# A linear-attention and bilinear-FFN kernel: first scores moved ahead of the last k transposes, and the second kv update of a pair moved next to its intra products

## The chip, the cores and the metric

One core of a Trainium2 chip runs the whole program. The metric is the time of one execution on the device, in microseconds (us); a version is described by the median of its runs.

## The reference, cut to what matters

The first half is linear attention with a decay per head, over 4 sequences of 768 tokens, 8 heads of 64; the second half is a feed-forward layer that multiplies two projections.

```python
# per sequence b and head h, token i (state kv is 64 x 64)
#   out = (q k^T * decay_mask) v   +   q * lam^(i+1) @ kv          "intra" + "inter"
#   kv  = lam^block * kv + (k * decay)^T v                         "kv update"
x = out.transpose(0, 2, 1, 3).reshape(3072, 512)
a = x @ w_a          # 512 x 1536
b = x @ w_b
y = (a * b) @ w_out  # 1536 x 512
```

The kernel works in units of 128 tokens, 24 in all, six to a sequence. The powers of lam are multiplied into q and k beforehand, so that the mask is a plain triangle and the kv state a plain running sum in PSUM.

## The kernel before

The FFN runs over groups of units. The attention of later units is cut into pieces that are put, by a table of slots, between the FFN's matmuls: `P` scales and loads, `T` transposes, `S` makes scores and masks, `V` is a kv update with its copy, `Q` is two older units' products with the next two units' scores, `O2` the same without scores.

```python
for _g, _u in ((3, 11), (4, 15), (5, 19)):
    PLAN.setdefault(_g, []).extend(
        [(1, "V", _u - 1), (1, "P", _u + 2), (3, "P", _u + 3), (4, "V", _u),
         (7, "Q", (_u, _u + 1, _u + 2, _u + 3)), (10, "V", _u + 1), (10, "P", _u + 4),
         (12, "P", _u + 5), (13, "V", _u + 2), (16, "Q", (_u + 2, _u + 3, _u + 4, _u + 5))])
# ... cut ...
def ps_bank(name, shape, dt, hold=False, ffn=False):   # seven PSUM banks, taken in rotation
    i = bank["next"]
    while i in bank["held"] or (ffn and i == bank["ffn"]):
        i = (i + 1) % 7
    # ... cut: remember i, bank["next"] = (i + 1) % 7, return a tile in bank i
# ... cut ...
def mask(kq):                       # two score banks -> two masked bf16 tiles, on DVE
    for i in range(2):
        m = msk_pool.tile([128, HP, 128], BF16, name=f"m{i}", tag=f"m{i}")
        nc.vector.tensor_mul(m, kq[i], lotri_bc)
# ... cut ...
def kv_mms(ps, w, hps, first):      # four 128 x 128 matmuls, a pair of heads each
    d = U[w]
    for hp in hps:
        nc.tensor.matmul(ps[:, hp, :, :], lhsT=d["kn"][:, 2 * hp:2 * hp + 2, :],
                         rhs=d["vb"][:, 2 * hp:2 * hp + 2, :], ...)
def kv_copy(u, ps, eng="dve"):      # the state to bf16, only the diagonal 64 x 64 blocks
    st = st_bufs[u % 4]
    if eng == "act":
        for i in range(2):
            p = slice(64 * i, 64 * i + 64)
            nc.scalar.copy(st[p, :, i, :], ps[p, :, i, :])
    else:
        nc.vector.tensor_mul(st..., ps..., bdiag_bc)
# ... cut ...
def pieces_O(us, nxt=()):
    kqs = [score_banks() for u in nxt]
    for u in us:
        inter(u)
    for u, kq in zip(nxt, kqs):
        scores(u, kq)
    for u in us:
        intra(u)
        xT, col = xTs[u]
        evac_o(u, xT, col)
    for u, kq in zip(nxt, kqs):
        masks(u, kq)
# ... cut; the head, for the first four units:
scores4(0)                          # after all k transposes
natural_k((0, 1, 2), (0, 1)); warm(2)
natural_k((0, 1, 2), (2, 3)); warm(2)
scores4(1); warm(4)
sts = [ps_bank("kv0", ...), ps_bank("kv1", ...), kv_bank()]
for hh in range(2):
    for u, ps in enumerate(sts):
        ...                         # kv parts, state copies of 0 and 1 on ACT, of 2 on DVE
```

## Time and profile before

| | before |
|---|---|
| median of its runs | 237.72 us |
| span of the profiled execution | 235.4 us |
| busy share of PE, DVE, ACT, POOL | 96%, 49%, 39%, 21% |

PE is TensorE, PEld its weight loads, DVE VectorE, ACT ScalarE, POOL GpSimd. In a timeline, a row is a run of like instructions: start, length, engine, line and operation, the tile written and those read, shapes, count, and in brackets how long the engine sat idle before it and what ended that. The lines themselves stand in the prediction. The profiled execution took 237.14 us, 0.6 less than the median, which matters for differences of a few tenths.

### The profile page before, as it was taken

How to read it: one execution, taken by the hardware profiler on the slowest of the kernel's cores; microseconds unless marked ns; L12 is line 12 of the kernel's file. 1: busy time of each engine (PE TensorE's matmuls, PEld its weight loads, DVE VectorE, ACT ScalarE, POOL GpSimd, SP SyncE). 2: the span in 40 equal slices, each digit the busy share in tenths (PEclk: the TensorE clock that was granted, in tenths of full speed). 3: DMA queues.
4: the chain of work that ended last, by engine and by line, in shares of the span. 5: the costliest groups of instructions: out<-in, count | busy, mean ns of one | idle time of the engine just before them, and what ended most of it. 6: DMA issues, size and time to landing. Idle time of an engine off the chain costs nothing.

```text
span 235.4 us, 4530 instructions
## 1 busy us (share of the span) xinstructions
PE 225.1 (96%) x1755; PEld 126.2 (54%) x1778; DVE 115.7 (49%) x205; ACT 92.9 (39%) x174; POOL 49.4 (21%) x63
## 2 busy tenths in 40 slices
PE   7699999998999999999999999999999999999994
PEld 2475444448698654444544454544454544444493
DVE  0886566637469637565135665135564215332050
ACT  3567654065565542341142241242341242431161
POOL 6041000245346453103306403003300000000000
PEclk9999999999999999999999999999999999999999
DMA  4999999999999999998919959523120220000311
GB/s 153 301 287 349 349 367 284 292 213 286 204 234 204 223 183 257 183 187 152 242 72 220 177 70 239 140 77 79 26 47 0 89 89 5 0 0 3 133 46 49
DMA packets 94278, 38.32 MB, mean 163 GB/s; under 512 B 81200, under 2 KB 89776, under 8 KB 94256
## 3 DMA queue, kind: packets, MB, share of 16 engines
q1 hardware_dynamic: 94112, 38.02, 71.0%
q8 instruction: 14, 0.23, 0.4%
q14 instruction: 8, 0.07, 0.1%
q10 hardware_dynamic: 144, 0.00, 0.0%
HBM read 28.32 MB, written 6.29 MB: 147 GB/s over the span
## 4 chain that ended last, share of the span: by engine, by line
PE 85%; DMA 6%; DVE 2%; ACT 2%; issue 2%; SPq 1%; DVEq 0%; ACTq 0%
PE op L434 26%; PE a_ps L413 25%; PE b_ps L413 24%; DMA k<-in_k_dram 3%; DMA qkT<-qk 3%; PE o_ps L345 2%; PE kq L308 2%; DVE m L320 2%; PE kvd L359 2%; PE o_ps L335 1%; PE tps L294 1%; ACT xT L352 1%; ACT o_sb L429 1%; SPq L206 1%; ACT st L379 1%
## 5 line engine op out<-in xcount | busy, mean ns | idle before, releaser
L425 DVE TENSOR_TENSOR ab<-a_sb,b_ps 128x512 bf16<-128x512 bf16 (+2 forms) x96 | 52.7, 553 | 82.3 <-PE b_ps L413 61.2
L413 PE MATMUL a_ps<-xT,wa_sb 128*128 128x512 bf16 (+2 forms) x378 | 76.7, 325 | 1.6 <-DVE ab L425 0.6
L413 PE MATMUL b_ps<-xT,wb_sb 128*128 128x512 bf16 (+2 forms) x379 | 76.7, 325 | 0.2
L420 ACT CAST a_sb<-a_ps 128x512 bf16<-128x512 f32 (+2 forms) x96 | 45.6, 481 | 65.6 <-PE a_ps L413 63.4
L434 PE MATMUL op<-wo_sb,ab 128*128 128x512 bf16 (+2 forms) x300 | 64.2, 362 | 0.9 <-issue 0.5
L413 PEld LDWEIGHTS <-wb_sb 128*128 128x128 bf16 x384 | 34.5, 98 | 28.7
L413 PEld LDWEIGHTS <-wa_sb 128*128 128x128 bf16 x384 | 33.5, 98 | 28.2 <-issue 1.6
L434 PEld LDWEIGHTS <-ab 128*128 128x128 bf16 x312 | 28.6, 98 | 30.2
L320 DVE TENSOR_TENSOR m<-kq,lotri 128x512 bf16<-128x512 f32 x48 | 29.9, 683 | 20.5 <-PE kq L308 19.6
L256 POOL TENSOR_TENSOR qk<-kf,lp_k 128x512 bf16<-128x512 f32 x17 | 17.9, 1053 | 76.9 <-issue 31.4
L429 ACT COPY o_sb<-op 128x512 f32<-128x512 f32 (+2 forms) x26 | 14.2, 554 | 37.2 <-PE op L434 36.7
L261 POOL TENSOR_TENSOR qk<-qf,lp_q 128x512 bf16<-128x512 f32 x20 | 23.1, 1154 | 23.8 <-DMA qf<-in_q_dram 23.8
L352 ACT CAST xT<-o_ps 128x512 bf16<-128x512 f32 x23 | 12.4, 590 | 16.9 <-PE o_ps L345 16.9
L381 DVE TENSOR_TENSOR st<-kvd,bdiag 128x512 bf16<-128x512 f32 x18 | 12.3, 684 | 3.8 <-PE kvd L359 3.8
L296 ACT COPY qkT<-tps 128x1024 bf16<-128x1024 bf16 x7 | 7.1, 1012 | 10.9 <-PE tps L294 10.9
L270 DVE CAST vb<-vf 128x512 bf16<-128x512 f32 x17 | 8.4, 496 | 0.0
L194 PE MATMUL idle<-idle_sb 128*128 128x128 bf16 (+1 forms) x38 | 7.2, 322 | 1.3 <-DVE idle_sb L189 1.3
L345 PE MATMUL o_ps<-m,vb 128*64 128x128 bf16 x192 | 7.8, 222 | 0.0
L270 POOL CAST vb<-vf 128x512 bf16<-128x512 f32 x7 | 4.3, 613 | 15.5 <-DMA vf<-in_v_dram 13.8
L308 PE MATMUL kq<-qkT 64*128 64x128 bf16 x160 | 6.7, 218 | 0.3 <-DMA qkT<-qk 0.3
L335 PEld LDWEIGHTS <-st 128*128 128x128 bf16 x80 | 5.4, 98 | 2.8
L345 PEld LDWEIGHTS <-vb 128*64 128x64 bf16 x192 | 5.7, 109 | 1.4
(52 smaller groups left out, 85.3 us busy)
## 6 DMA issues: line engine op xcount, KB each, us to landing
vf<-in_v_dram SPq DMA_DIRECT2D x24, 256.0 KB, 5.2
out_dram<-o_sb SPq DMA_DIRECT2D x23, 256.0 KB, 2.3
qf<-in_q_dram SPq DMA_DIRECT2D x20, 256.0 KB, 4.5
kf<-in_k_dram SPq DMA_DIRECT2D x20, 256.0 KB, 5.1
wst<-in_moe_w_a_dram SPq DMA_DIRECT2D x6, 512.0 KB, 8.7
wst<-in_moe_w_b_dram SPq DMA_DIRECT2D x6, 512.0 KB, 8.8
wst<-in_moe_w_out_dram SPq DMA_DIRECT2D x6, 512.0 KB, 8.5
q<-in_q_dram SPq DMA_DIRECT2D x2, 512.0 KB, 5.4
```

The lines of the kernel that those rows point to most:

```text
L256: eng_of(eng).tensor_mul(qk[:, 1], raw.pop((u, "k")), lp_k[:, u % NB].to_broadcast([128, H, D]))
L261: eng_of(eng).tensor_mul(U[u]["qk"][:, 0], raw.pop((u, "q")), lp_q[:, u % NB].to_broadcast([128, H, D]))
L270: eng_of(eng).tensor_copy(vb, vf)
L320: nc.vector.tensor_mul(m, kq[i], lotri_bc)
L345: nc.tensor.matmul(d["o"][p, hp, :], lhsT=d["vb"][:, 2 * hp + i, :], rhs=d["m"](i, hp), start=(first and hp == 0), stop=True, skip_group_c ...
L352: nc.scalar.copy(xT[:, :, col:col + BLK], o_ps)
L381: nc.vector.tensor_mul(st[:].rearrange("p hp i d -> p hp (i d)"), ps[:].rearrange("p hp i d -> p hp (i d)"), bdiag_bc)
L413: nc.tensor.matmul(ps[:, :gt], lhsT=w_sb[:, s, f * 128:(f + 1) * 128], rhs=xT[:, s, :gt], start=(s == 0), stop=(s == KS - 1))
L420: nc.scalar.copy(a_sb[:, :gt], ps[:, :gt])
L425: nc.vector.tensor_mul(ab[:, f, :gt], a_sb[:, :gt], ps[:, :gt])
L429: nc.scalar.copy(o_sb[:, lo:hi], op[:, lo:hi])
L434: nc.tensor.matmul(op[:, lo:hi], lhsT=ab[:, f, t * 128:(t + 1) * 128], rhs=wo_sb[:, f, lo:hi], start=(f == 0), stop=(f == FC - 1))
```

## The change

Two intents. In the head, the scores of the first heads no longer stand behind the last k transposes, so that the masks, which follow one another without a gap, start sooner. From the pair (7, 8) on, the kv update of a pair's second unit moves next to its intra products. For six of the eight units both then use half of PE's columns (column tiling): eight matmuls of 64 columns compute only the blocks that are kept, instead of four of 128 whose off-diagonal half the copy throws away. Units 12 and 18, the first of their sequences, keep the four full matmuls.

```diff
-        [(1, "V", _u - 1), (1, "P", _u + 2), (3, "P", _u + 3), (4, "V", _u),
-         (7, "Q", (_u, _u + 1, _u + 2, _u + 3)), (10, "V", _u + 1), (10, "P", _u + 4),
+        [(1, "P", _u + 2), (3, "P", _u + 3), (4, "V", _u),
+         (7, "Q", (_u, _u + 1, _u + 2, _u + 3)), (10, "P", _u + 4),
 # ... cut: V of 8 and 22 go from groups 2 and 6, S of 11 and 12 from slot 2 to 3
+    def kv_beside(u):
+        if u % NB == 0 or u % NB == NB - 1:
+            kv_update(u)
+        for hp in range(HP if 0 < u % NB < NB - 1 else 0):
+            for i in range(2):
+                p = slice(64 * i, 64 * i + 64)
+                nc.tensor.matmul(kv["ps"][p, hp, i, :], lhsT=U[u]["kn"][:, 2 * hp + i, :],
+                                 rhs=U[u]["vb"][:, 2 * hp + i, :],
+                                 start=False, stop=True, skip_group_check=True)
+        if u % NB < NB - 1:
+            kv_copy(u, kv["ps"])
 # pieces_O
             evac_o(u, xT, col)
+        if len(us) == 2 and us[0] >= n0 + 3:
+            kv_beside(us[1])
         for u, kq in zip(nxt, kqs):
             masks(u, kq)
 # ... cut: load4 is split into scale4, transpose4, part_k; scores4 takes the pairs to do
-    scores4(0)
+    scores4(0, (0, 1))
+    part_k(1, 1)
     natural_k((0, 1, 2), (0, 1))
 # ... cut
-    scores4(1)
-    warm(4)
# ... cut: the old loop over hh goes; kv_part(u, hps) adds up units 0 to u in sts[u]
+    scores4(1, (0,))
+    kv_part(0, (0, 1))
+    kv_part(1, (0, 1))
+    scores4(1, (1,))
+    kv_part(2, (0, 1))
+    for u in range(2):
+        kv_part(u, (2, 3))
+        kv_copy(u, sts[u], "act")
     intra(0)
     evac_o(0, *xTs[0])
     intra(1)
+    kv_part(2, (2, 3))
+    kv_copy(2, sts[2], "dve")
```

## The prediction

> **What bounds the kernel now.** I read the page first, then the chain of work that ended last, then the timelines of PE, DVE and ACT around the places that the diff touches. From the page, busy times and the chain:
>
> ```profile
> span 235.4 us, 4530 instructions
> ...
> PE 225.1 (96%) x1755; PEld 126.2 (54%) x1778; DVE 115.7 (49%) x205; ACT 92.9 (39%) x174; POOL 49.4 (21%) x63
> ...
> PE 85%; DMA 6%; DVE 2%; ACT 2%; issue 2%; SPq 1%; DVEq 0%; ACTq 0%
> ```
>
> PE is the bound. After the first FFN matmul at 19.35 us its idle gaps sum to about 1.6 us (0.63 at 57.46, 0.30 at 101.60 on a DMA transpose, four of 0.16 to 0.17). So whatever delays PE goes straight into the time, and only PE work taken away, or one of these gaps, can be won. DVE is half idle, but its order matters where PE waits for a PSUM bank that DVE has to read first. Timeline of PE, then of DVE, in one four-unit piece (older pair (15, 16), next pair's scores (17, 18)) inside the a/b matmuls of group 4:
>
> ```profile
> 136.15 0.61 PE L335 MATMUL o_ps<-qkT,st 128*128 128x128 bf16 x8
> 136.70 0.62 PE L308 MATMUL kq<-qkT 64*128 64x128 bf16 x16
> 137.25 0.64 PE L345 MATMUL o_ps<-m,vb 128*64 128x128 bf16 x16
> 137.87 1.02 PE L413 MATMUL a_ps<-xT,wa_sb 128*128 128x512 bf16 x3
> ...
> 136.42 0.69 DVE L425 TENSOR_TENSOR ab<-a_sb,b_ps 128x512 bf16<-128x512 bf16 x1 [1.04 <-PE b_ps L413]
> 137.13 2.48 DVE L320 TENSOR_TENSOR m<-kq,lotri 128x512 bf16<-128x512 f32 x4
> ```
>
> The reader should see that a_ps starts at 137.87 when the first of four masks (0.684 us each, starting every 0.60) ends at 137.81. In the built program that a_ps takes the bank of the first score tile and waits for its mask: this piece is already at its limit. The end of the head, timelines of DVE, ACT and PE:
>
> ```profile
> 12.52 3.68 DVE L320 TENSOR_TENSOR m<-kq,lotri 128x512 bf16<-128x512 f32 x6 [0.89 <-PE kq L545]
> ...
> 15.52 1.88 DVE L320 TENSOR_TENSOR m<-kq,lotri 128x512 bf16<-128x512 f32 x3
> ...
> 17.31 0.68 DVE L381 TENSOR_TENSOR st<-kvd,bdiag 128x512 bf16<-128x512 f32 x1
> ...
> 18.05 0.62 PE L335 MATMUL o_ps<-scratch,st 128*128 128x128 bf16 x8
> ...
> 19.35 1.89 PE L413 MATMUL a_ps<-xT,wa_sb 128*128 128x512 bf16 x7 [0.46 <-ACT xT L352]
> ```
>
> Eight masks without a gap (12.52 to 17.40), the state copy to 17.99, the inter products, the last xT copy on ACT to 19.29, then the FFN: the mask chain sets the FFN's start.
>
> **What the Trainium skill says.** "TensorEngine Tiling (Array Packing)", Key Properties: changing the tiling mode drains TensorE. The trace agrees: 16 half-array matmuls occupy 0.55 us and 8 of them 0.33 (100.58 to 101.93, without the DMA wait), so 0.027 each plus 0.11 per change of mode. The same page, Instruction Overhead: a free dimension below some 60 columns saves nothing, about 60 cycles are paid anyway. The kernel before has no 64-column matmul, so its trace doesn't show it. "PSUM — Partial Sum Buffer", PSUM bank collisions raise a hardware error: guard PSUM by bank, not by address. The 0.06 us between mask end and a_ps above is such a guard. "TensorE: Matmul & The Clock Gate", Architectural detail: ScalarE and VectorE queues are strict FIFO; in the DVE timeline nothing overtakes. That carries this prediction.
>
> **The change part by part.**
>
> (a) kv updates of units 8, 10, 12, 14, 16, 18, 20, 22 move from their own slots to just after the intra products. Removed: eight groups of four matmuls such as the one at 107.69 us, each displacing the next a_ps by 0.22 us (107.69 to 107.91). Added: for 12 and 18 (first of a sequence) the same four full matmuls; for the other six, eight 128*64 matmuls of 64 columns. I take the intra products' 0.027 each, 0.22 in all, as the low columns may hit the fixed overhead; at best 0.11. So PE work alone: 0 to -0.7 us, centre -0.1. The mode change back to 128*128 is paid in either kernel.
>
> (b) The order on DVE. In the built program the state copy of the second unit now stands ahead of the four masks of the next pair, and it waits for kv matmuls that come after all intra products. Call the start of the inter products T0.
> - Before: scores done about T0+0.95, masks from T0+0.98, a_ps at T0+1.72.
> - After, units 16 and 20 (groups 4 and 5): intra starts T0+1.10, kv at T0+1.53, last kv result T0+1.53+0.19+0.22=1.94, copy at 1.98 or a little sooner, first mask 0.60 later at about 2.55, ends 3.23, a_ps (same wait in the built program) about T0+3.26. That is +1.54, less 0.22 for the removed update: **+1.32 each**.
> - Unit 12 (group 3): only one inter product, so intra starts at T0+0.87, ends 1.30; mode change 0.13, four full matmuls, done 1.82; copy 1.86, mask 2.46 to 3.14, a_ps T0+3.20. Before it was T0+1.92 (100.58 to 102.50), 0.30 of that being the DMA wait, which I expect gone because PE comes later. +1.28-0.22: **+1.06**.
> - The three pieces among output matmuls (units 14, 18, 22) have 1.3 us of held-bank op matmuls before they need the first mask's bank (needed T0+3.35, free 3.27): 0.
> - Group 2, unit 8. The next pair (9, 10) follows soon: inter(10) needs the state of 9, whose copy stands on DVE behind four masks and a vb cast:
>
> ```profile
> 79.96 2.48 DVE L320 TENSOR_TENSOR m<-kq,lotri 128x512 bf16<-128x512 f32 x4 [1.81 <-PE kq L308]
> 82.36 0.42 DVE L270 CAST vb<-vf 128x512 bf16<-128x512 f32 x1
> 82.69 0.68 DVE L381 TENSOR_TENSOR st<-kvd,bdiag 128x512 bf16<-128x512 f32 x1
> ...
> 83.47 0.61 PE L335 MATMUL o_ps<-qkT,st 128*128 128x128 bf16 x8
> ```
>
>   Before, that copy ends at 83.37, just in time. After, from T0 = 78.98 less 0.22: copy of 8 at T0+1.95, masks from 2.55, cast at 4.96, copy of 9 from 5.29 to 5.97, inter(10) at T0+6.03; before it was 83.69, T0+4.71. +1.32-0.22: **+1.10**. Moving the scores of 11 and 12 one slot later is worth 0: they waited for nothing.
>
> (c) The head. The first scores no longer wait for the last k transposes (11.69): they can start at 11.60 against 12.02, so the masks start 0.42 earlier, at 12.10, the fourth ending at 14.60. But the bank rotation shifts: scores of the second half now take the banks of masks 3 and 4 and wait for both, so they start at 14.65, and mask 5 at 15.11 after a gap of 0.5; mask 8 ends 17.62 against 17.40. Behind 14.65 PE runs 8 scores, 6 kv, 8 scores, 6 kv, 2 kv with three changes of mode: 0.22+0.11+0.33+0.11+0.22+0.11+0.33+0.11 = 1.54, so the first state copy on ACT starts near 16.40 (was 16.19). Then intra(1) waits for that bank (two copies of 0.38: 17.20), kv of unit 2 to 17.86, inter(1), intra(2, 3), inter(2, 3) with two changes of mode to about 19.17, last result 19.35, ACT copy 0.59, FFN at about 20.0: **+0.65**. The four warming matmuls dropped there save nothing: PE waits anyway.
>
> (d) POOL and DMA. The qk buffer for unit 12 is freed by the update of unit 8, about 4 us later than before, but its transpose was issued only at 85.90 (POOL had been done at 80.2), so that is hidden. The other moved updates free their buffers earlier, also hidden.
>
> Sum: -0.1+1.32+1.32+1.06+1.10+0.65 = **+5.35 us**; 237.72+5.35 = 243.1.
>
> **The rivals.**
> - The intended gain: PE work falls by 0.7 us and the head by 0.4, giving 236.6. For it: PE is 96% busy and the masks do start earlier. Against it: the a_ps wait, which leaves no slack at 137.81 to 137.87.
> - The delays are half absorbed: DVE is half idle and POOL/DMA sets some waits, such as the 6.23 us transpose ahead of 101.60. Then about +2.5, 240.2. Against it: after 101.6 there is no PE idle left to absorb into, and queues are in order.
> - A new DMA bound: PE later by 2 us before group 3 delays stores on the same queue and with them the transposes. The DMA share is 0.9 and more up to 106 us, so it could cost another us: 244.2. Against it: the transposes of 13 and 14 were held by the backlog of loads, not by PE.
>
> **Range and chances.** The three a/b stalls are firm (instruction order and measured durations), say +-0.2 each; unit 8's +-0.3; the head is the weakest, -0.4 to +1.0. Together 241.7 to 244.3 for 8 in 10. The 2% line is 242.5, 0.6 below my centre: slower by over 2% 0.74, within 2% 0.23, faster 0.03.
>
> **What would show each step.** (b) In groups 3 to 5, PE idle of 1.2 to 1.4 us before an a_ps, released by a mask on DVE, and a state copy ahead of the four masks; idle of about 1.1 us before the inter products of (9, 10), released by a state copy. (a) The 64-column kv groups: 0.1 to 0.22 us from first to next. (c) First FFN matmul near 20.0, masks in two blocks of four with a 0.5 us gap. The prediction is wrong if a_ps takes another bank than the first mask's, if the eight 64-column matmuls cost far over 0.25 us, or if the head starts the FFN before 19.35.

## The result, and the profile after

The changed kernel took 243.11 us in the median (243.02 to 243.55), the kernel before 237.72 beside it (237.71 to 237.79). The ratio is 1.023, with an interval of 1.0212 to 1.0248: slower by over 2%. A ratio is the mean time of one kernel's fast runs over that of the other's of the same rounds, so not quite the ratio of the medians quoted.

The page after, busy times and the chain of work that ended last:

```profile
span 241.3 us, 4568 instructions
...
PE 227.1 (94%) x1798; PEld 125.7 (52%) x1798; DVE 116.0 (48%) x205; ACT 92.7 (38%) x174; POOL 47.9 (20%) x63
...
PE 87%; DVE 5%; DMA 3%; ACT 2%; issue 1%; SPq 1%; DVEq 0%; ACTq 0%
```

No engine has over 2 us more to do than before, yet the span grew by 5.9. (Six groups of four matmuls became eight and four warming matmuls went: 20 more, as the weight loads count. PE's own count grows by 43, since the trace before lacks the records of 23 matmuls.) DVE's share of the chain went from 2% to 5%: it is not busier, PE waits for it. Of that growth some 0.5 us belongs to the executions and not to the change: the medians differ by 5.39, the profile of before is of a fast execution, and in the trace after PE falls back by a further 0.4 us from 74.1 to 75.8 us, for a reason that looks like chance and is told with the two halves below. The granted clock was lower (0.997 against 1.000) only in the last 6 us, when PE's work ends.

The waits of PE after, in us, times, longest. Neither line is among the waits before:

```profile
PE a_ps L427 <- DVE m L320: 4.2, 3, 1.4
...
PE o_ps L335 <- DVE st L393: 1.0, 1, 1.0
```

and of its weight loads, also new:

```profile
PEld L448 <- DVE m L320: 1.1, 2, 0.6
```

This line is of the pieces of units 14 and 18, among the output matmuls (L448). Matmuls count as busy until a modelled end, so a short wait hides in PE's own rows; the starts show it. Output matmuls start 0.216 us apart, but 0.37 us at 122.59 and 0.47 at 159.08, each just after the end of the piece's first mask (122.53 and 159.02): 0.15 and 0.25 us lost.

The piece in group 4 that the prediction showed, now, timeline of PE:

```profile
139.22 0.61 PE L335 MATMUL o_ps<-qkT,st 128*128 128x128 bf16 x8
139.76 0.62 PE L308 MATMUL kq<-qkT 64*128 64x128 bf16 x16
140.32 0.64 PE L345 MATMUL o_ps<-m,vb 128*64 128x128 bf16 x16
140.79 0.29 PE L380 MATMUL kvd<-vb,qk 128*64 128x64 bf16 x8
142.47 1.04 PE L427 MATMUL a_ps<-xT,wa_sb 128*128 128x512 bf16 x4 [1.39 <-DVE m L320]
```

and of DVE:

```profile
141.12 0.69 DVE L393 TENSOR_TENSOR st<-kvd,bdiag 128x512 bf16<-128x512 f32 x1 [0.94 <-PE kvd L380]
141.73 2.47 DVE L320 TENSOR_TENSOR m<-kq,lotri 128x512 bf16<-128x512 f32 x4
```

The first unit's scores were done by about 140.2 (0.98 us after the inter products began, when the masks started before), but the first mask starts only at 141.73, behind a state copy that itself waited 0.94 us for the kv matmuls. Its end is at about 142.41, and a_ps starts at 142.47 in the bank that this mask reads. From the start of the inter products to a_ps it was 1.72 us and is now 3.25.

Group 2, timelines of PE and of DVE, answering to the lines from 79.96 to 83.47 before:

```profile
84.34 0.39 PE L335 MATMUL o_ps<-qkT,st 128*128 128x128 bf16 x4
85.71 0.40 PE L335 MATMUL o_ps<-qkT,st 128*128 128x128 bf16 x4 [0.98 <-DVE st L393]
```

```profile
81.62 0.69 DVE L393 TENSOR_TENSOR st<-kvd,bdiag 128x512 bf16<-128x512 f32 x1 [2.88 <-PE kvd L380]
82.23 2.48 DVE L320 TENSOR_TENSOR m<-kq,lotri 128x512 bf16<-128x512 f32 x4
84.62 0.43 DVE L270 CAST vb<-vf 128x512 bf16<-128x512 f32 x1
84.97 0.68 DVE L393 TENSOR_TENSOR st<-kvd,bdiag 128x512 bf16<-128x512 f32 x1
```

The copy of unit 8 (81.62) pushes back the masks, these the cast, and the cast the copy of unit 9 (84.97), for which the inter products of unit 10 wait. The head, DVE:

```profile
12.06 2.48 DVE L320 TENSOR_TENSOR m<-kq,lotri 128x512 bf16<-128x512 f32 x4 [0.46 <-PE kq L560]
14.98 2.48 DVE L320 TENSOR_TENSOR m<-kq,lotri 128x512 bf16<-128x512 f32 x4 [0.44 <-PE kq L560]
```

and PE:

```profile
20.07 1.24 PE L427 MATMUL a_ps<-xT,wa_sb 128*128 128x512 bf16 x5 [0.45 <-ACT xT L352]
```

The masks start 0.46 us sooner than before (12.06 against 12.52) and then come apart in the middle; the first FFN matmul starts at 20.07 (before 19.35).

### The profile page after: what moved, and what is told of

Its sections match the earlier page's. It is cut to its first block, busy times and chain, and to the rows that moved or that the text cites. A ratio compares the mean times of both kernels' runs of the same rounds, so it can differ in the third digit from the quotient of the medians.

```text
span 241.3 us, 4568 instructions
## 1 busy us (share of the span) xinstructions
PE 227.1 (94%) x1798; PEld 125.7 (52%) x1798; DVE 116.0 (48%) x205; ACT 92.7 (38%) x174; POOL 47.9 (20%) x63
## 4 chain that ended last, share of the span: by engine, by line
PE 87%; DVE 5%; DMA 3%; ACT 2%; issue 1%; SPq 1%; DVEq 0%; ACTq 0%
PE a_ps L427 26%; PE b_ps L427 26%; PE op L448 24%; DMA k<-in_k_dram 3%; DVE m L320 3%; PE o_ps L345 3%; PE kq L308 2%; PE o_ps L335 2%; DVE st L393 1%; PE kvd L359 1%; PE tps L294 1%; ACT o_sb L443 1%; SPq L206 1%; ACT xT L352 0%; PE kq L560 0%
## 5 line engine op out<-in xcount | busy, mean ns | idle before, releaser
L448 PE MATMUL op<-wo_sb,ab 128*128 128x512 bf16 (+2 forms) x312 | 65.9, 363 | 0.1
L448 PEld LDWEIGHTS <-ab 128*128 128x128 bf16 x312 | 28.5, 98 | 30.5 <-DVE m L320 1.1
L261 POOL TENSOR_TENSOR qk<-qf,lp_q 128x512 bf16<-128x512 f32 x20 | 21.7, 1084 | 24.2 <-DMA qf<-in_q_dram 24.2
L335 PE MATMUL o_ps<-qkT,st 128*128 128x128 bf16 x68 | 5.8, 219 | 1.0 <-DVE st L393 1.0
```

What stands on the lines that cost most here:

```text
L261: eng_of(eng).tensor_mul(U[u]["qk"][:, 0], raw.pop((u, "q")), lp_q[:, u % NB].to_broadcast([128, H, D]))
L335: nc.tensor.matmul(d["o"][:, hp, :], lhsT=st_bufs[(u - 1) % 4][:, hp, :, :], rhs=d["qT"][:, hp, :], start=(first and hp == 0), stop=True, ...
L448: nc.tensor.matmul(op[:, lo:hi], lhsT=ab[:, f, t * 128:(t + 1) * 128], rhs=wo_sb[:, f, lo:hi], start=(f == 0), stop=(f == FC - 1))
```

## The experiments

All outputs are right.

### The masks ahead of the state copy

```diff
         if u % NB < NB - 1:
-            kv_copy(u, kv["ps"])          # in kv_beside
 # pieces_O
         for u, kq in zip(nxt, kqs):
             masks(u, kq)
+        if len(us) == 2 and us[0] >= n0 + 3 and us[1] % NB < NB - 1:
+            kv_copy(us[1], kv["ps"])
```

> The changed kernel with one edit: in a piece the four masks of the next pair are emitted ahead of the state copy (the kv matmuls stay next to the intra products). Theory (the order on DVE is the cause): the three waits of 1.38 to 1.39 us before a_ps in groups 3, 4 and 5 shrink to 0.1 us or less (-4.1 us), and in group 2 the inter products of units 9 and 10 come about 0.4 us earlier, less than the full 1.3, because the kv update of unit 9 then has to wait until the copy of unit 8 has read the same bank: 238.6 us (238.1 to 239.0). Rival A (the kv matmuls and mode changes in the piece cost the time themselves): 242.5 us or more. Rival B (the later copy starves the next update or inter product about as much as it helps): about 240.5 us.

Measured: 238.14 us, ratio 1.0028 (1.0005 to 1.0050). PE in group 4 and, last line, in group 2:

```profile
139.57 0.29 PE L380 MATMUL kvd<-vb,qk 128*64 128x64 bf16 x8
139.80 1.04 PE L427 MATMUL a_ps<-xT,wa_sb 128*128 128x512 bf16 x3
```

```profile
84.48 0.38 PE L359 MATMUL kvd<-vb,qk 128*128 128x128 bf16 x4 [0.85 <-DVE st L391]
```

All three waits before a_ps are gone, and so are those of the weight loads in the pieces of units 14 and 18, with the kv matmuls where the change put them: the theory holds and rival A falls. In group 2 the wait moved, as expected: the update of unit 9 now waits 0.85 us for the later copy of unit 8. It is a small piece of rival B.

### The state copy on ScalarE

```diff
-            kv_copy(u, kv["ps"])
+            kv_copy(u, kv["ps"], "act")   # in kv_beside, still ahead of the masks
```

> The changed kernel, but the state copy next to the intra products is made by ScalarE (two copies of 64 partitions, 0.37 us each) instead of DVE; it is still emitted ahead of the masks. Theory (only the place in DVE's queue hurts, not the kv work nor its place in the program): the three waits of 1.39 us before a_ps and the one of 1 us in group 2 go, 5.2 us less: 237.9 us (237.4 to 238.6, part of it for ScalarE, whose a_sb copies now come 0.7 us later). Rival (the copy costs the time wherever it is made): 241 us or more.

Measured: 237.25 us, ratio 0.9991 (0.9976 to 1.0005): 5.9 us under the changed kernel by the medians, where 5.2 was expected; the waits of 0.15 and 0.25 us in the pieces of units 14 and 18, which the expectation did not count, went too. The profiled execution was this kernel's slowest (239.89 us; its first products start 2.1 us late, see below), so it is read within the piece, here PE and then ACT in group 4:

```profile
139.18 0.61 PE L335 MATMUL o_ps<-qkT,st 128*128 128x128 bf16 x8
...
140.97 1.04 PE L427 MATMUL a_ps<-xT,wa_sb 128*128 128x512 bf16 x3
```

```profile
140.73 1.07 ACT L352 CAST xT<-o_ps 128x512 bf16<-128x512 f32 x2 [1.63 <-PE o_ps L345]
141.69 0.75 ACT L391 CAST st<-kvd 64x256 bf16<-64x256 f32 x2
142.46 0.59 ACT L434 CAST a_sb<-a_ps 128x512 bf16<-128x512 f32 x1
```

The inter products to a_ps take 1.79 us, and a_sb 0.7 us later does not hold PE up. No wait for a mask or a state copy is left in groups 2 to 5. From group 2 to the end this trace's distance from before shrinks from 3.53 to 2.65 us, by 0.88; 0.3 of that is the DMA wait of group 3, which it does not have, and the other 0.6 is close to the 0.7 us of PE work that the intended gain counted on (in the trace; the time's interval reaches over 1). So neither the kv work nor its place costs anything; its copy's place in DVE's queue does. The program order did not change here: only the engine did.

### Unit 8 back in its old slot

```diff
-        (6, "S", 8), (7, "V", 7), (8, "P", 10), (9, "T", 9), (11, "T", 10),
+        (6, "S", 8), (7, "V", 7), (8, "P", 10), (9, "T", 9), (10, "V", 8), (11, "T", 10),
# ... cut; pieces_O:
-        if len(us) == 2 and us[0] >= n0 + 3:
+        if len(us) == 2 and us[0] >= n0 + 5:
```

> The changed kernel with one part undone: unit 8 is updated in its old slot, with four full matmuls. Theory: the wait of about 1 us before the inter products of units 9 and 10 goes and 0.22 us of kv matmuls come back: -1.05 us, ratio to before lower by 0.0044 than the changed kernel's 1.023, 242.1 us (241.7 to 242.5), with the three waits of 1.39 us left. Rival (the wait moves to the next place in group 2): 242.9 us or more.

Measured: 242.47 us, ratio 1.0206 (1.0192 to 1.022), lower by 0.0024 and not 0.0044, with intervals that overlap: the time alone does not tell the theory from the rival. The traces do. From the transposes of unit 9 before the piece to the output matmuls after the products of unit 10, this kernel loses 0.11 us on before and the changed kernel 1.17, a difference of 1.06, as sized; the wait of 0.98 is gone, and the three of 1.39 stand. The profiled execution lost 0.24 us elsewhere, earlier than the piece.

### Four full matmuls instead of eight column-tiled ones

```diff
-        if u % NB == 0 or u % NB == NB - 1:
-            kv_update(u)
-        for hp in range(HP if 0 < u % NB < NB - 1 else 0):
+        kv_update(u)
+        for hp in ():
```

> The changed kernel, but the moved kv updates are always four full 128-column matmuls, never eight column-tiled ones. Theory (column tiling itself is a gain, eight 64-column matmuls take about 0.13 us): units 8, 16 and 20 get their kv result 0.2 us later (0.09 more work, 0.11 for the change of mode that now comes before it), units 10, 14 and 22 0.09 us more PE work: +0.87 in all, 244.0 us (243.6 to 244.2). Rival (what the prediction assumed: eight of 64 columns cost the same 0.22 us as four of 128): only the change of mode ahead of the copy in three pieces, +0.3, 243.4 us.

Measured: 244.7 us, ratio 1.0298 (1.0273 to 1.0322). That is 1.6 us over the changed kernel by the medians and 1.3 by the traces, more than the 0.87 expected; 0.28 of it arises ahead of the first edited piece, and 0.13 in the piece of unit 14, whose output matmuls wait that much longer for the first mask. The piece in group 4, PE:

```profile
140.00 0.61 PE L335 MATMUL o_ps<-qkT,st 128*128 128x128 bf16 x8
...
141.66 0.40 PE L359 MATMUL kvd<-vb,qk 128*128 128x128 bf16 x4
143.44 1.04 PE L426 MATMUL a_ps<-xT,wa_sb 128*128 128x512 bf16 x3 [1.38 <-DVE m L320]
```

From the inter products to a_ps it is 3.44 us against 3.25, the 0.2 that was expected: the matmuls start 0.09 later (1.66 against 1.57 after the inter products; a change of mode comes first), and the copy another 0.10 later after them. So column tiling is a gain in itself, and the prediction's 0.22 us for eight such matmuls was too much. Where nothing waits (139.57 to 139.80 in the masks-first run) a_ps starts 0.23 after them, with a change of mode of 0.11 in it that the intra products pay anyway, and from the last intra product to the next full matmul it is 0.276 us with the eight in between and 0.152 without: so eight add about 0.12 us, or 0.016 each. Their starts show how: they come in pairs 3 to 4 ns apart, one in each column half, and the pairs 25 to 29 ns apart.

### The two halves of the change, each alone

The head alone is the kernel before with the new head; the kv part alone is the changed kernel with the old head.

```diff
# head alone: only the hunks from load4 to kv_copy(2, sts[2], "dve")
# kv alone:   only the hunks of PLAN, kv_beside and pieces_O
```

> The kernel before with only the new head (first scores ahead of the last k transposes, new order of the kv parts). Theory (head costs by the rotation of the banks): first FFN matmul at 20.07 us instead of 19.35, time +0.6 to +0.7, 238.4 us (238.2 to 238.6). Rival A (the head is a gain when nothing else changes): 237.3 us. Rival B (later idle absorbs the head's delay): 237.8 us.

> The new head alone once more, with more rounds, since the first time gave a ratio of 1.0001 with an interval of 0.4% where +0.65 us (1.0027) was expected. Theory (the delay of 0.72 us at the start of the FFN shrinks only where PE waits in group 1 for the scaling of k on DVE, by 0.1 to 0.5): ratio 1.001 to 1.0025, 237.9 to 238.3 us. Rival (all of it is absorbed): ratio 0.9995 to 1.0005.

> The changed kernel with the head of the kernel before. Theory (the two parts add up): 243.11 less 0.65, 242.5 us (242.2 to 242.8), with the same three waits of about 1.39 us before a_ps and about 1 us before the inter products of unit 10. Rival (the delays hide each other in part): 243.0 us or more, or below 241.5 us.

| run | median us | ratio to before (95%) | first FFN matmul |
|---|---|---|---|
| head alone | 237.72 | 1.0001 (0.9979 to 1.0023) | 20.07 |
| head alone, again | 238.43 | 1.0029 (0.9996 to 1.0062) | 20.19 |
| kv part alone | 242.79 | 1.0210 (1.0181 to 1.0239) | 19.37 |

The kv part alone holds nearly all of the loss, with the same waits as in the changed kernel. Of the head alone, the first run fits its rival B (237.8) and the second, 238.43, lies just above the theory's range. The head's delay of 0.72 us at the first FFN matmul is there each time, but what of it reaches the end is not sharp: nothing in the first run, 0.7 in the second, 0.3 to 0.4 from the two together, 0.5 from the difference of 1.023 and 1.021. A likely reason for the scatter lies at 57 us, where PE waits for a product of a and b that stands on DVE behind the scaling of k for unit 6. That scaling, in the kernel before (DVE, then POOL):

```profile
56.17 1.04 DVE L256 TENSOR_TENSOR qk<-kf,lp_k 128x512 bf16<-128x512 f32 x1
```

```profile
55.62 1.04 POOL L256 TENSOR_TENSOR qk<-kf,lp_k 128x512 bf16<-128x512 f32 x1 [1.40 <-DMA kf<-in_k_dram]
```

and in the masks-first run:

```profile
56.92 1.57 DVE L256 TENSOR_TENSOR qk<-kf,lp_k 128x512 bf16<-128x512 f32 x1
```

```profile
56.91 1.04 POOL L261 TENSOR_TENSOR qk<-qf,lp_q 128x512 bf16<-128x512 f32 x1
```

The same instruction takes 0.68 us alone and here 0.90 to 1.57, ending about 0.55 after the GpSimd product that had begun before it (56.66 to 57.21; 57.95 to 58.49). This agrees with the Trainium skill, "SBUF — State Buffer", Who interferes with whom: DVE with two SBUF inputs and GpSimd share a port pair, and the pair is an exclusive lock. No run took GpSimd's work away, so the lock is argued from the overlap. GpSimd mostly starts when a load lands, so the overlap differs from run to run, and PE's wait is 0.4 us less than the scaling's length, from 0.3 to 1.2 us in these traces.

There is a second such place. Ahead of the masks of units 7 and 8, DVE casts a v tile, in the kernel before and, second, in the changed kernel, where a GpSimd product (71.69 to 72.73) lies beside it:

```profile
71.43 0.42 DVE L270 CAST vb<-vf 128x512 bf16<-128x512 f32 x1
```

```profile
72.01 1.01 DVE L270 CAST vb<-vf 128x512 bf16<-128x512 f32 x1
```

In the changed kernel three matmul groups start just as the second, third and fourth mask end (74.60, 75.20, 75.80), and PE falls back by 0.4 us. The cast took 0.42 to 0.67 us in four profiles, where nothing was lost (before, its control, the first run with other banks, mended), and 0.71 to 1.21 in the other ten, where PE lost about its length less 0.62. A shift of 0.7 us before these two places can come out as anything from nothing to more than itself.

### The kernel before once more

> A control: the kernel before, unchanged, to see how far two sets of its own runs and two of its own profiles differ. The one profile of before that the prediction used is of a run at 237.14 us, 0.6 us faster than its median. Theory (that profile caught a lucky execution): this profile spans about 236.0 us instead of 235.4, and the extra time lies at the scaling of k for unit 6 on DVE in group 1 (1.04 us then; 0.68 alone; up to 1.57 in other runs while GpSimd works beside it), so PE's wait at 57 us is over 0.9 us. Rival: the 0.6 us is spread over short gaps with a lower granted clock. Ratio 1.000 within 0.001 either way.

Measured: 237.55 us (237.13 to 238.59), ratio 0.9994 (0.9966 to 1.0023). The profile fell on one of the two fastest runs again (237.14 us, span 235.4), in which the scaling took 0.68 us and PE waited 0.3. So the theory was not met in this profile, and neither is the rival: why most executions of before take some 0.5 us more than its two profiled ones stays open (a longer cast at 72 us, as above, would do it, but no slower run of before was profiled). It does show that two profiles of this kernel, of equally long runs, differ by up to 0.3 us on the way, and that a set of six runs is good to about 0.3%. Two later profiles, of runs at 239.3 (the head with other banks) and 239.9 us (the copy on ScalarE), had their lateness at the start: the power table on DVE starts at 6.87 and 6.72 us instead of 4.6, since the logarithm of lam was late.

### The head with other banks

```diff
-            kq = score_banks()
+            kq = given or score_banks()       # in scores4
+    bank["next"] = 2
+    kq2 = [score_banks(), score_banks()]      # ahead of the kv tiles
     sts = [ps_bank("kv0", ...), ps_bank("kv1", ...), kv_bank()]
-    scores4(1, (0,))
+    scores4(1, (0,), kq2[0])
 # and the same for scores4(1, (1,)) with kq2[1]; FFN and kv part as before
```

> The new head alone, with one edit: the score tiles of its second half take the banks of the transposed k, free at 13.8 and 14.5 us, and the first kv tiles take those of masks 2 and 3. Theory (the rotation of the banks is what costs, since those scores wait for masks 3 and 4): eight masks without a gap from 12.06 to about 17.0 us, state copies on ACT from about 15.7, first FFN matmul at 18.9 us (18.7 to 19.1), that is 1.1 us earlier than with the new head as it is and 0.45 earlier than before; time 0.2 to 0.5 us under before. Rival (the new order of the kv parts is what costs): first FFN matmul stays near 20.0 us.

> The new head with the other banks once more, as the base for the next run on the same chip. First FFN matmul at 18.85 us again; ratio 0.994 to 0.997 to before.

Measured: 236.59 us, ratio 0.9952 (0.9923 to 0.9981), then 237.21 us, ratio 0.9992 (0.9959 to 1.0025). The timelines of DVE and of PE:

```profile
12.08 4.88 DVE L320 TENSOR_TENSOR m<-kq,lotri 128x512 bf16<-128x512 f32 x8 [0.45 <-PE kq L546]
```

```profile
18.85 1.46 PE L413 MATMUL a_ps<-xT,wa_sb 128*128 128x512 bf16 x5 [0.45 <-ACT xT L352]
```

Eight masks in one row, and the FFN starts at 18.85 us, 1.22 earlier than with the new head as it is: the rotation of the banks was the cause, and the new order of the kv parts, unchanged here, was not. The second profile was of this kernel's slowest run (239.33 us, a late start), so its 21.39 says nothing on the head. In time the gain is 0.5% in one set and nothing sure in the other, which missed the expected 0.994 to 0.997: both sets hold runs near 236.1 and near 237.5.

### Mended versions

The mended kernel has the head's other banks, the masks ahead of the copy, and unit 8 in its old slot. The second version keeps units 12 and 18 in their old slots too, so that only the five column-tiled updates move.

```diff
# mended: the three edits above, all together
# five tiled: and
-        if len(us) == 2 and us[0] >= n0 + 5:
+        if len(us) == 2 and us[0] >= n0 + 5 and us[1] % NB:
# with (10, "V", 12) and (1, "V", 18) back in PLAN
```

> The changed kernel with three mends: the head's other banks, the masks ahead of the state copy in every piece, and unit 8 updated in its old slot. Theory: the head 0.45 us earlier than before (in part lost again in group 1), seven kv updates next to the intra products save 7 x 0.22 - 5 x 0.13 - 2 x 0.22 = 0.45 us, no wait of 1.4 us before a_ps and none of 1 us in group 2: 236.8 us (236.2 to 237.2), 0.4 to 1.2 us under before. Rival (the later state copies hold up kv updates or inter products as the one of unit 9 did in the masks-first run): 237.5 us or more.

> The head with the other banks, and of the kv updates only the five column-tiled ones that gain something (units 10, 14, 16, 20, 22) next to the intra products, masks ahead of the state copy; units 8, 12 and 18 in their old slots. Theory (column tiling: a group adds 0.10 to 0.13 us instead of 0.22): 5 x 0.1 = 0.5 us less than the run with the other banks alone on the same chip (0.3 to 0.6), 236.1 us. Rival (the pieces lose it again to waits, as in the mended kernel): same as the other banks alone within 0.1 us.

Measured: 236.84 us, ratio 0.9975 (0.9932 to 1.0018), and 236.81 us, ratio 0.9971 (0.9950 to 0.9992). The second is the only one of the two whose interval lies below 1. The waits of the changed kernel are gone from both. In the mended trace the second score group of group 3 waits 0.6 us for a transposing DMA, which ate over half of the 0.6 us that tiling saved; the prediction's kernel before had 0.3 there. In the trace of the five tiled ones the distance to the run with other banks alone falls by 0.51 us from group 2 to the end, the expected 5 x 0.1, but the times do not resolve it (236.81 against 237.21, both sets scattered over 1.4 us and more). ScalarE's copy together with the head's other banks was not run.

## Why the prediction was right

The time (243.1 predicted, 243.11 measured) and the side of the 2% line came out. The terms, read as how far the changed trace falls behind the trace before across each place:

| term | predicted | in the traces | tested by |
|---|---|---|---|
| (a) kv work of units 10, 14, 18, 22 | -0.1 | about -0.3 | full matmuls |
| (b) units 16 and 20 | +1.32 each | +1.32 each | masks first, copy on ScalarE |
| (b) unit 12 | +1.06 | +1.08 | the same |
| (b) unit 8 | +1.10 | +1.04 | unit 8 in its old slot |
| (b) waits among the output matmuls, units 14 and 18 | 0 | +0.15 and +0.25 | masks first, copy on ScalarE |
| (c) head | +0.65 | +0.72 at the FFN's start, -0.14 at 57 us | head alone, other banks |
| (d) POOL and DMA | 0 | no new wait | - |

The right column of numbers sums to +5.4; with the 0.4 us at 74 us, which is not put down to the change, that is the 5.9 by which the traces differ, and the medians differ by 5.39. The agreement to a hundredth is luck: the waits of units 14 and 18 that the prediction left out (0.4) and the kv work and the head that it set too high (0.2 and 0.1) nearly cancel, and two sets of runs of one kernel differ by more.

Step (b), which carried the result, is shown by two edits that each took the three waits before a_ps away in a different manner, and by a third that took away unit 8's alone. The places where the prediction put these waits, their releasers and their lengths (1.2 to 1.4 us; 1.38 to 1.39 measured) were right, and so was the removal of the DMA wait in group 3 of the changed kernel. DVE kept its order in every trace: in group 4 a mask whose scores were ready stood 1.5 us behind a copy whose matmuls were not. The half-absorbed rival (240.2) and the DMA rival (244.2) fall: but for the DMA wait of 0.3 us in group 3, which the prediction counted in, and 0.14 us of the wait at 57 us, no idle absorbed the delays, and no new wait for a transfer appears. The intended gain did exist: with the copy on ScalarE it shows in the trace, though the times do not resolve it.

One part of (b) failed: it had the output matmuls of units 14, 18 and 22 need the first mask's bank at T0+3.35, after its release at T0+3.27. In the trace (T0 is the start of the inter products) they were due at T0+3.09 (unit 14) and T0+2.97 (unit 18), ahead of the mask's end at T0+3.19 and T0+3.16; only unit 22, with two masks and not four, did not wait. A reading failed too, without consequence: three of the prediction's four idle gaps of 0.16 to 0.17 us are missing matmul records (at 118.22 the matmul before has its weight load at 117.99 and no record of its own).

Step (a) was mis-sized. It took the intra products' 0.027 us for each 64-column matmul, 0.22 for eight, on the ground of a fixed cost per matmul. The traces have about 0.016 each and 0.12 for eight. The step that failed is the floor: it was counted for each matmul in turn, although the two column halves work side by side (starts in pairs 3 to 4 ns apart), as 0.027 for a 128-column intra product had already shown (half of the 0.055 of a full one). The Trainium skill, "TensorEngine Tiling (Array Packing)", Key Properties, says that tiles operate independently; that should have been read with its section on overhead, and 0.016 agrees with it. The term is small because in units 8, 12, 16 and 20 the kv matmuls are counted in (b), in the chain ahead of the copy.

Step (c) was right in its mechanism and size at the FFN's start (20.0 predicted, 20.07 measured). What it left out is that the wait at 57 us, which it listed among PE's gaps, is of a length that varies by itself, and that PE can wait at 74 us as well; how much of the 0.72 us reaches the end is therefore not settled better than 0 to 0.7.

## What to carry to other kernels

When work moves next to other work on one engine, look at what follows it on the others: here the matmuls were cheap, but their evacuation entered an in-order queue ahead of instructions that the next matmul's bank depended on. Emit first what frees the bank that PE needs next, or give the late evacuation to an engine that is not on that path. Where buffers rotate, reordering their users also changes who waits for whom; the assignment has to be looked up again after each such move.

## What the Trainium skill lacked or had wrong

- "TensorE: Matmul & The Clock Gate", Wait — 56ns, not 53.3ns?: start-to-start is said never to drop below about 25 ns. Here the 64-column matmuls of the two column halves start 3 to 4 ns apart, and only the pairs keep 25 to 29 ns, so that eight add 0.12 us, about 16 ns each. The same page's part on packing has such starts about 4 ns apart; the sentence on the floor does not except them.
- "TensorEngine Tiling (Array Packing)": Key Properties names the drain at a change of mode without a size, which is about 0.11 us in these traces. Instruction Overhead gives about 60 cycles for each matmul and does not itself say that these overlap across tiles, as the same 16 ns show.
- "SBUF — State Buffer" has the lock that DVE and GpSimd share, but no figure for what it costs two products of this kind: 0.90 to 1.57 us in the runs for a DVE product that takes 0.68 alone.
